# First pass over the tokens with two weight slices instead of three, weight conversions moved behind the masks of the attention pairs, q of units 1 and 3 decayed on GpSimd

## Chip, core and metric

The kernel runs on one core of one Trainium2 chip. The metric is device time in microseconds, the median of several executions. A profiled execution gives a trace of every instruction of the engines: TensorE (PE, its weight loads as PEld), VectorE (DVE), ScalarE (ACT), GpSimd (POOL) and SyncE (SP), which issues the DMAs.

## What is computed

Three layers, one behind the other, in float32:

```python
# q, k, v: (4, 8, 576, 64); x: (2304, 512) after the first layer
scores = q @ k.transpose(0, 1, 3, 2) / sqrt(64)
ret = scores * gamma[head] ** (i - j)        # for i >= j, else 0; no softmax
x = (ret @ v)                                # heads side by side: (2304, 512)
h = x @ w_in                                 # (2304, 2048)
x = (h * sigmoid(1.702 * h)) @ w_out         # (2304, 512)
h = x @ w2_in                                # (2304, 1024)
s = h * softmax(h)
out = ((s - mean(s)) / sqrt(var(s) + 1e-6) * g_ln) @ w2_out
```

## The kernel before

Every matmul of the two feed-forward layers is made of three: each operand is split into a high part (rounded to fp32r, by ScalarE) and a remainder (operand minus high part, by GpSimd or VectorE), and high x high, low x high and high x low are summed in PSUM. The weights come as 64 bit floats; VectorE turns them into 32 bit floats with three bit instructions per half slice (`convert`, lines 236, 239, 242: a shift, and two combinations), ScalarE rounds (L279 for a half, L259 for a whole slice), GpSimd subtracts (L283, L264).

**Attention.** 16 units (a batch and two heads each) run as 8 pairs `k`; at the end of pair `k` the raw weight halves and the x splits for the first block are issued. Of a pair: `scores` (L399 on PE, then the masks on VectorE, L404), `states` (L363) and `scan` (L372), `across` (L429 to L441: earlier chunks through the scanned states), `within` (L414), and `take`, which brings the result into `xb`. q has to be multiplied by powers of gamma: for units from `PLAIN` = 4 on GpSimd does it ahead (`decay_q`, L333, L338) and `take` is a ScalarE copy (L452); for units 0 to 3 `take` multiplies on VectorE instead (L457, L459), with `qdec` for even and `odec` for odd units.

**First feed-forward layer.** The 2304 tokens are five blocks `j` of 384, 512, 512, 512 and 384 columns, the hidden size is 16 slices `f` of 128. `GENS` cuts the slices into passes: in pass `g` all five blocks run through the slices of that pass, and the outputs of the passes are added up in `y`. A step (g, j, f) is an h group (`emit_h`: 12 matmuls, L496, then sigmoid on ScalarE L501, product L504, rounding L508 or L506, remainder L509) and a y group (`emit_y`: 12 matmuls, L529). PE's order is h of the next step, then y of the step before. h0_2 below is the h group of block 0 and slice 2. x of the next block is split in the last two steps of a block (`split_x`, L476 on ScalarE, L477 on GpSimd): of four parts two in the last step but one, two in the last.

**The order of background work** is written out by hand: `self.bg` is a list of pieces (conversions count 1, the roundings and remainders behind them 0); `background(n)` takes n conversions and what follows them off the list and puts them into the engines' queues at that place. In the pairs the table `(0, 0, 0, 0, 0, 1, 2, 3)[k]` and one further call say how many; in the steps `bg` and `free`. Each engine runs its queue in order, so a piece stands still when one ahead of it waits. `load_w` issues the next raw half slice on SP; `halves` is the order of the first six (slices 0, 1 and 2).

**Later.** While the first layer runs, the slices 8 to 15 and the second layer's weights are loaded, converted and split in the same way; the second layer follows.

Of the kernel before, what the change touches and what calls it, by code (L numbers as in the profile page):

```python
# [17 lines left out]
B, H, S, D = 4, 8, 576, 64  # L18
NP = H // 2
# [13 lines left out]
FH = NF // 2  # L33
GENS = ((0, 3), (3, 8), (8, 16))
STEPS = [(g, j, f) for g, lo_hi in enumerate(GENS) for j in range(NB) for f in range(*lo_hi)]
# [14 lines left out]
for _name, _w in (  # L50
    ("half", 1), ("g_ln", FB), ("vdec", NP * 3), ("step", NP), ("istep", H), ("tri2", LAST), ("tri", CH),
    ("qdec", NP * CH), ("odec", NP // 2 * CH),
):
    _CC[_name] = (_n, _n + _w)
    _n += _w
# [4 lines left out]
def constants():  # L60

    gamma = (1.0 - 2.0 ** (-5.0 - np.arange(H))).astype(np.float64)
    c = np.zeros((P, _n_consts), np.float64)

    def put(name, a):
        lo, hi = _CC[name]
        c[:, lo:hi] = a.reshape(P, hi - lo)

    qdec = np.zeros((P, NP, CH))
    odec = np.zeros((P, NP // 2, CH))  # L70
    step = np.zeros((P, NP))
    vdec = np.zeros((P, NP, 3))
    j = np.arange(P)
    for p in range(NP):

        g = gamma[2 * p + (j // D ^ p % 2)]
        qdec[:, p] = g[:, None] ** j[None, :]
        step[:, p] = g ** CH
        for a in range(2):
            vdec[:, p, a] = gamma[2 * p + a] ** (CH - j)  # L80
        vdec[:, p, 2] = g ** -(j % D)
        if p % 2:
            odec[:, p // 2] = gamma[2 * p + j // D][:, None] ** j[None, :]
    put("qdec", qdec)
    put("odec", odec)
    put("step", step)
    put("istep", np.broadcast_to(gamma ** -CH, (P, H)))

    put("vdec", vdec / math.sqrt(D))
    put("tri", (j[:, None] <= np.arange(CH)[None, :]).astype(np.float64))  # L90
    put("tri2", (j[:, None] % D <= np.arange(LAST)[None, :]).astype(np.float64))
    put("half", np.full((P, 1), -0.5))
    return c.astype(np.float32)
# [25 lines left out]
NU = 6  # L119
PLAIN = 4  # L120
EARLY = 3
# [35 lines left out]
class Build:  # L157
# [38 lines left out]
    def load_decays(self, p, n):  # L196

        lo = _CC["qdec"][0] + p * CH
        hi = lo + n * CH if p + n < NP else CCONST
        self.load(_M["c"] + lo, self.const_in[:, lo:hi])  # L200

# [124 lines left out]

    def decay_q(self, k):

        n = NCH * CH
        for u in (2 * k, 2 * k + 1):  # L330
            q = self.un(u)[0][:, CQ:CK]
            d = self.const("qdec")[:, u % NP * CH:(u % NP + 1) * CH]
            self.nc.gpsimd.tensor_tensor(q[:, n:], q[:, n:], d[:, 0:LAST], ALU.mult)  # L333
        for u in (2 * k, 2 * k + 1):
            q = self.un(u)[0][:, CQ:CK]
# [110 lines left out]
    def take(self, u, o, part):  # L446
# [3 lines left out]
        x = self.x(u)[:, n:S] if part else self.x(u)[:, 0:n]  # L450
        if u >= PLAIN:
            nc.scalar.copy(x, o[:, 0:LAST] if part else o)  # L452
            return
        p = u % NP
        d = self.const("odec")[:, p // 2 * CH:] if p % 2 else self.const("qdec")[:, p * CH:]
        if part:
# [246 lines left out]
    def run(self):  # L703
# [15 lines left out]
        for f in range(FH):  # L719
            self.wraw[f] = self.wp.tile([P, 2 * SLICE], U32, tag="w", name=f"wraw{f}", bufs=FH)  # L720
        halves = [(0, 0), (1, 0), (0, 1), (2, 0), (1, 1), (2, 1)]
        raws = halves + [(f, h) for f in range(3, FH) for h in range(2)]

# [7 lines left out]
        self.load_unit(0, 1)  # L731
        self.load_decays(0, 1)
        self.fill_scan()
        for u in range(1, NU):
            for part in range(2):
                self.load_unit(u, part)
            if u == 2:
                self.load_decays(1, NP - 1)

        for f, h in halves:  # L740
# [3 lines left out]
            self.bg += [(0, p, "split") for p in self.split_half(f, t, h)]  # L744
        for f in range(3, FH):
            t = T_START[f % 2]
# [7 lines left out]
        self.scale_v(0)  # L754
        self.scale_v(1)
        for k in range(NPAIR):
            u = 2 * k
            nxt = k + 1 < NPAIR
            early = k < EARLY
            if k + 2 < NPAIR:  # L760
                self.decay_q(k + 2)
            if nxt and not early:
# [66 lines left out]
        for g, j, f in STEPS:  # L829
# [222 lines left out]
```

## Time and profile before

| | us |
|---|---|
| median of 3 runs | 688.37 (688.34 to 688.55) |
| profiled execution | 687.97 |
| its span, first to last instruction | 686.2 |
| PE busy in the span | 666.3 (97%) |
| DVE busy | 487.6 (71%) |
| POOL busy | 250.5 (37%) |
| ACT busy | 231.8 (34%) |

The profiled execution took 687.97 us, 0.4 less than the median; 1.8 us of it lie around the span. Sums below are made against the profiled execution. A share of busy time is a mean over stages with different limits: attention takes about the first 67 us, the first feed-forward layer runs until about 480, the second until the end. Matmuls are pipelined, so a busy PE need not be at full rate: PEclk says what clock it was granted.

### The profile page before, as it was taken

Reading aid. Unit: us, or ns where it says so; the run is one execution under the profiler, and the core shown is the slowest. Engines: PE = TensorE matmul, PEld = TensorE weight load, DVE = VectorE, ACT = ScalarE, POOL = GpSimd, SP = SyncE. Lnnn points to the kernel's source line nnn. Section 1 sums busy time; section 2 is a strip of 40 time slices with the busy share of each in tenths; the row PEclk is TensorE's granted clock in tenths of the full one; section 3 lists DMA queues with packets and bytes.
Section 4 is the critical chain, followed back from the end, with each engine's and each line's share of the span. In section 5 each row is a group of like instructions: output and inputs, shape, how many; then the busy total and the mean of one; then the engine's idle time right before and its main releaser. Section 6 shows DMA issues by size and latency. Waiting matters only on the chain.

```text
span 686.2 us, 10467 instructions
## 1 busy us (share of the span) xinstructions
PE 666.3 (97%) x4086; PEld 577.0 (84%) x4086; DVE 487.6 (71%) x773; ACT 231.8 (34%) x494; POOL 250.5 (37%) x264
## 2 busy tenths in 40 slices
PE   9999779999999999999999999999999999999998
PEld 8898658899788889898888888899888888888887
DVE  3768546777978869768677676458789887877780
ACT  2554324443121114311121211155754434452331
POOL 1444624643442217912040220259943224331300
PEclk9999889999999999999999999999999999999999
DMA  8996330000212222013211110000000000000001
GB/s 334 416 399 265 124 123 1 0 2 1 90 64 93 92 93 62 0 32 96 90 62 62 62 32 0 1 1 4 1 16 1 32 32 31 32 16 16 32 31 47
DMA packets 14881, 49.48 MB, mean 72 GB/s; under 512 B 1648, under 2 KB 2288, under 8 KB 14832
## 3 DMA queue, kind: packets, MB, share of 16 engines
q1 hardware_dynamic: 14832, 48.82, 19.8%
q8 instruction: 32, 0.52, 0.3%
q14 instruction: 17, 0.14, 0.1%
HBM read 44.09 MB, written 4.72 MB: 71 GB/s over the span
## 4 chain that ended last, share of the span: by engine, by line
PE 80%; DVE 7%; issue 6%; POOL 5%; ACT 1%; POOLq 0%; DVEq 0%; ACTq 0%
PE yp L529 24%; PE h L496 24%; PE o L694 14%; PE h L603 10%; POOL xs L477 3%; POOL w L264 2%; PE zT L667 2%; PE s L399 2%; PE o L429 1%; PE o L414 1%; PE warm L714 1%; PE T L363 1%; DVE mem L404 1%; DVE mem L609 1%; DVE mem L504 1%
## 5 line engine op out<-in xcount | busy, mean ns | idle before, releaser
L529 PE MATMUL yp<-gs,w 128*128 128x512 f32 (+1 forms) x960 | 215.7, 373 | 10.3 <-ACT w L279 7.3
L496 PE MATMUL h<-xs,w 128*128 128x512 f32 (+1 forms) x960 | 214.0, 370 | 2.2 <-POOL xs L477 2.0
L529 PEld LDWEIGHTS yp<-gs,w 128*128 128x128 f32 x960 | 177.9, 191 | 35.6 <-ACT w L279 8.1
L496 PEld LDWEIGHTS h<-xs,w 128*128 128x128 f32 x960 | 176.3, 189 | 28.5 <-POOL xs L477 5.2
L477 POOL TENSOR_TENSOR xs<-xb,xs 128x384 fp32r<-128x384 f32 (+3 forms) x96 | 94.2, 1009 | 203.1 <-ACT xs L476 203.1
L501 ACT ACTIVATE mem<-h 128x512 f32<-128x512 f32 (+1 forms) x80 | 44.5, 556 | 269.9 <-PE h L496 265.4
L504 DVE TENSOR_TENSOR mem<-h,mem 128x512 f32<-128x512 f32 (+1 forms) x80 | 50.9, 636 | 101.9 <-ACT mem L501 101.8
L694 PE MATMUL o<-w,zs 128*128 128x512 f32 (+1 forms) x456 | 102.9, 382 | 0.0
L694 PEld LDWEIGHTS o<-w,zs 128*128 128x128 f32 x456 | 81.3, 188 | 15.2
L509 DVE TENSOR_TENSOR gs<-mem,gs 128x512 fp32r<-128x512 f32 (+1 forms) x80 | 68.4, 855 | 13.9 <-ACT gs L506 6.9
L264 POOL TENSOR_TENSOR w<-mem,w 128x512 fp32r<-128x512 f32 x34 | 46.0, 1381 | 36.3 <-ACT w L259 36.3
L565 POOL TENSOR_TENSOR ys_s<-mem,ys_s 128x256 fp32r<-128x256 f32 x36 | 35.1, 986 | 51.9 <-ACT ys_s L564 41.8
L508 DVE CAST gs<-mem 128x512 fp32r<-128x512 f32 (+1 forms) x69 | 38.9, 563 | 6.9 <-PE yp L529 0.5
L603 PE MATMUL h<-wt,ys_s 128*128 128x512 f32 x162 | 41.3, 390 | 0.0
L609 DVE TENSOR_TENSOR mem<-h,mem 128x512 f32<-128x512 f32 x36 | 24.6, 687 | 21.1 <-PE h L603 12.5
L603 PEld LDWEIGHTS h<-wt,ys_s 128*128 128x128 f32 x162 | 30.3, 188 | 6.2
L476 ACT CAST xs<-xb 128x384 fp32r<-128x384 f32 (+3 forms) x96 | 35.0, 433 | 0.0
L654 POOL TENSOR_TENSOR mem<-mem 128x1 f32<-128x1 f32 x18 | 10.3, 574 | 64.7 <-DVE mem L653 64.7
L404 DVE SCALAR_TENSOR_TENSOR mem<-s,mem 128x512 f32<-128x512 f32 x32 | 21.8, 739 | 9.8 <-PE s L399 9.8
L677 DVE TENSOR_TENSOR zs<-zT,zs 128x512 fp32r<-128x512 f32 x36 | 23.1, 684 | 7.7 <-ACT zs L676 7.7
L603 PE MATMUL h<-wb,ys_a 128*128 128x512 f32 x108 | 27.5, 390 | 0.3 <-ACT mem L612 0.3
L646 DVE TENSOR_TENSOR mem<-mem 128x1024 f32<-128x1024 f32 x18 | 24.8, 1375 | 3.7 <-ACT mem L644 3.7
(82 smaller groups left out, 726.0 us busy)
## 6 DMA issues: line engine op xcount, KB each, us to landing
mem<-in_att SPq DMA_DIRECT2D x16, 576.0 KB, 8.2
mem<-in_att SPq DMA_DIRECT2D x16, 544.0 KB, 9.0
wraw<-in_w SPq DMA_DIRECT2D x16, 512.0 KB, 10.0
mem<-in_w SPq DMA_DIRECT2D x16, 512.0 KB, 3.7
out<-mem SPq DMA_DIRECT2D x17, 256.0 KB, 2.0
mem<-in_w2in SPq DMA_DIRECT2D x8, 512.0 KB, 3.7
mem<-in_w2out SPq DMA_DIRECT2D x8, 512.0 KB, 3.6
mem<-in_consts SPq DMA_DIRECT2D x1, 320.0 KB, 8.9
```

The costliest lines, as they stand in the source:

```text
L264: nc.gpsimd.tensor_tensor(lo[:, c], w[:, c], f32(hi[:, c]), ALU.subtract)
L476: nc.scalar.copy(t[:, 0, done:done + n], x)
L477: nc.gpsimd.tensor_tensor(t[:, 1, done:done + n], x, f32(t[:, 0, done:done + n]), ALU.subtract)
L496: nc.tensor.matmul(h[:, 0:width], a[:, w], x[:, b, 0:width], start=(n == 0), stop=(n == 3 * KB - 1))
L501: nc.scalar.activation(g, h[:, 0:width], AF.Sigmoid, scale=1.702)
L504: nc.vector.tensor_tensor(g, h[:, 0:width], g, ALU.mult)
L508: nc.vector.tensor_copy(gs[:, 0], g)
L509: lo_engine.tensor_tensor(gs[:, 1], g, f32(gs[:, 0]), ALU.subtract)
L529: nc.tensor.matmul(o, a[:, w], gs[:, b], start=(first and i == 0), stop=(last and i == 2))
L565: nc.gpsimd.tensor_tensor(ys[:, 1], src, f32(ys[:, 0]), ALU.subtract)
L603: nc.tensor.matmul(o, a[:, l, k], m[:, w], start=(start and i == 0), stop=(stop and i == 5), skip_group_check=True,)
L694: nc.tensor.matmul(o[:, 0:n], z[:, a, k], b[:, c:c + n], start=(k == 0 and i == 0), stop=(k == FB - 1 and i == 2),)
```

## The change

The first pass takes slices 0 and 1, the second slices 2 to 7, the third 8 to 15 as before. Only the four halves of slices 0 and 1 are converted one by one, three conversions in each of the pairs 4 to 7, behind that pair's masks. In the first pass two conversions follow each h group and one each y group; the last two x parts are queued directly behind the last h group. Of units 0 to 3 only 0 and 2 are still multiplied in `take`; q of units 1 and 3 is decayed on GpSimd ahead of the pairs. `odec` goes, the decays of odd unit 1 are loaded ahead of those of unit 0. Raw slices are loaded in another rhythm (one half in pairs 2 to 5, three in pairs 6 and 7).

```diff
-GENS = ((0, 3), (3, 8), (8, 16))
+GENS = ((0, 2), (2, 8), (8, 16))
...
-PLAIN = 4
+PLAIN = (0, 2)
...
-    def decay_q(self, k):
+    def decay_q(self, *units):
...
-        if u >= PLAIN:
+        if u not in PLAIN:
             nc.scalar.copy(x, o[:, 0:LAST] if part else o)
             return
-        p = u % NP
-        d = self.const("odec")[:, p // 2 * CH:] if p % 2 else self.const("qdec")[:, p * CH:]
+        d = self.const("qdec")[:, u % NP * CH:]
...
-        halves = [(0, 0), (1, 0), (0, 1), (2, 0), (1, 1), (2, 1)]
-        raws = halves + [(f, h) for f in range(3, FH) for h in range(2)]
+        halves = [(0, 0), (1, 0), (0, 1), (1, 1)]
+        raws = halves + [(f, h) for f in range(2, FH) for h in range(2)]
...
-        self.load_decays(0, 1)
+        self.load_decays(1, 1)
         self.fill_scan()
         for u in range(1, NU):
             for part in range(2):
                 self.load_unit(u, part)
+            if u == 1:
+                self.load_decays(0, 1)
             if u == 2:
-                self.load_decays(1, NP - 1)
+                self.load_decays(2, NP - 2)
...
+        self.decay_q(1)
+        self.decay_q(3)
         for k in range(NPAIR):
...
             if k + 2 < NPAIR:
-                self.decay_q(k + 2)
+                self.decay_q(u + 4, u + 5)
...
-            self.background((0, 0, 0, 0, 0, 1, 2, 3)[k])
+            self.background((0, 0, 0, 0, 2, 2, 2, 3)[k])
...
-                self.background(k > 4)
+                self.background(k > 3)
                 self.scan(k + 1, pt)
...
-            for _ in range((0, 0, 1, 1, 2, 2, 1, 1)[k]):
+            for _ in range((0, 0, 1, 1, 1, 1, 3, 3)[k]):
                 load_w()
...
-                for _ in range(2):
+                for _ in range(3):
                     load_w()
...
-            if fl:
+            if g == 0:
+                while ahead and not start:
+                    ahead.pop(0)()
+                self.background(2)
+            elif fl:
                 self.background(bg, free)
...
-            self.background(1 if fl else 1 + bg, free and not fl)
+            if g:
+                self.background(1 if fl else 1 + bg, free and not fl)
+            else:
+                self.background(1)
```

What this does to the queues stands in the order of the built programs. In their rows `wraw1` is a raw slice, `w1` a split one, `mem` holds the converted half in between, `h0_1` is an h group's bank, `gs` its split result, `xs0_1_2` part 2 of block 1's x in pass 0.

VectorE from the end of attention on, before, from h0_0's product to h0_2's:

```order
L504 TENSOR_TENSOR mem_60<-h0_0_972,mem_60 128x384
L509 TENSOR_TENSOR gs_71<-mem_60,gs_71 128x384
L242 SCALAR_TENSOR_TENSOR mem_60<-wraw0_95 128x512
L236 TENSOR_SCALAR mem_60<-wraw2_97 128x512
L239 SCALAR_TENSOR_TENSOR wraw2_97<-wraw2_97,mem_60 128x512
L242 SCALAR_TENSOR_TENSOR mem_60<-wraw2_97 128x512
L504 TENSOR_TENSOR mem_60<-h0_1_1033,mem_60 128x384
L509 TENSOR_TENSOR gs_71<-mem_60,gs_71 128x384
L236 TENSOR_SCALAR mem_60<-wraw1_96 128x512
L239 SCALAR_TENSOR_TENSOR wraw1_96<-wraw1_96,mem_60 128x512
L242 SCALAR_TENSOR_TENSOR mem_60<-wraw1_96 128x512
L504 TENSOR_TENSOR mem_60<-h0_2_1073,mem_60 128x384
```

and with the change, from the last pair's conversions to h0_1's remainder:

```order
L231 TENSOR_SCALAR mem_60<-wraw1_96 128x512
L234 SCALAR_TENSOR_TENSOR wraw1_96<-wraw1_96,mem_60 128x512
L237 SCALAR_TENSOR_TENSOR mem_60<-wraw1_96 128x512
L498 TENSOR_TENSOR mem_60<-h0_0_985,mem_60 128x384
L503 TENSOR_TENSOR gs_71<-mem_60,gs_71 128x384
L231 TENSOR_SCALAR mem_60<-wraw2_97 128x512
L234 SCALAR_TENSOR_TENSOR wraw2_97<-wraw2_97,mem_60 128x512
L237 SCALAR_TENSOR_TENSOR mem_60<-wraw2_97 128x512
L231 TENSOR_SCALAR mem_60<-wraw2_97 128x512
L234 SCALAR_TENSOR_TENSOR wraw2_97<-wraw2_97,mem_60 128x512
L498 TENSOR_TENSOR mem_60<-h0_1_1046,mem_60 128x384
L503 TENSOR_TENSOR gs_71<-mem_60,gs_71 128x384
```

Before, the last conversion of slice 0 and all of the second halves of slices 1 and 2 stood behind the products of h0_0, h0_1 and h0_2. Now slice 1's last half stands ahead of h0_0's product, and what follows it is slice 2, which the first pass does not use.

GpSimd in the same place, before:

```order
L283 TENSOR_TENSOR w1_946<-mem_60,w1_946 128x512
L283 TENSOR_TENSOR w0_844<-mem_60,w0_844 128x512
L283 TENSOR_TENSOR w2_1018<-mem_60,w2_1018 128x512
L477 TENSOR_TENSOR xs0_1_0_1023<-xb_78,xs0_1_0_1023 128x192
L477 TENSOR_TENSOR xs0_1_0_1023<-xb_78,xs0_1_0_1023 128x320
L477 TENSOR_TENSOR xs0_1_1_1028<-xb_78,xs0_1_1_1028 128x192
L477 TENSOR_TENSOR xs0_1_1_1028<-xb_78,xs0_1_1_1028 128x320
L283 TENSOR_TENSOR w1_946<-mem_60,w1_946 128x512
L477 TENSOR_TENSOR xs0_1_2_1087<-xb_78,xs0_1_2_1087 128x192
L477 TENSOR_TENSOR xs0_1_2_1087<-xb_78,xs0_1_2_1087 128x320
L477 TENSOR_TENSOR xs0_1_3_1092<-xb_78,xs0_1_3_1092 128x192
L477 TENSOR_TENSOR xs0_1_3_1092<-xb_78,xs0_1_3_1092 128x320
```

and with the change:

```order
L278 TENSOR_TENSOR w0_697<-mem_60,w0_697 128x512
L471 TENSOR_TENSOR xs0_0_3_929<-xb_78,xs0_0_3_929 128x384
L278 TENSOR_TENSOR w1_813<-mem_60,w1_813 128x512
L471 TENSOR_TENSOR xs0_1_0_1029<-xb_78,xs0_1_0_1029 128x192
L471 TENSOR_TENSOR xs0_1_0_1029<-xb_78,xs0_1_0_1029 128x320
L471 TENSOR_TENSOR xs0_1_1_1034<-xb_78,xs0_1_1_1034 128x192
L471 TENSOR_TENSOR xs0_1_1_1034<-xb_78,xs0_1_1_1034 128x320
L471 TENSOR_TENSOR xs0_1_2_1060<-xb_78,xs0_1_2_1060 128x192
L471 TENSOR_TENSOR xs0_1_2_1060<-xb_78,xs0_1_2_1060 128x320
L471 TENSOR_TENSOR xs0_1_3_1065<-xb_78,xs0_1_3_1065 128x192
L471 TENSOR_TENSOR xs0_1_3_1065<-xb_78,xs0_1_3_1065 128x320
L259 TENSOR_TENSOR w2_1074<-mem_60,w2_1074 128x512 x2
```

The remainders of slices 0 and 1 now stand ahead of block 1's x; its eight subtractions follow each other, and slice 2's remainder comes behind them.

TensorE behind y0_0, before:

```order
L529 MATMUL yp0_0_3_1054<-gs_71,w0_844 128x384
L496 MATMUL h0_2_1073<-xs0_0_0_587,w2_1018 128x384 x3
L496 MATMUL h0_2_1073<-xs0_0_1_698,w2_1018 128x384 x3
L496 MATMUL h0_2_1073<-xs0_0_2_807,w2_1018 128x384 x3
L496 MATMUL h0_2_1073<-xs0_0_3_915,w2_1018 128x384 x3
```

and with the change:

```order
L523 MATMUL yp0_0_3_1082<-gs_71,w0_697 128x384
L490 MATMUL h1_0_1108<-xs0_1_0_1029,w0_697 128x512 x3
L490 MATMUL h1_0_1108<-xs0_1_1_1034,w0_697 128x512 x3
L490 MATMUL h1_0_1108<-xs0_1_2_1060,w0_697 128x512 x3
L490 MATMUL h1_0_1108<-xs0_1_3_1065,w0_697 128x512 x3
```

h1_0, which needs block 1's x, takes the place of h0_2.

## Rows read from the trace of the kernel before

**Rows 1.** Page, the span in 40 slices: PE's busy tenths.
```profile
PE   9999779999999999999999999999999999999998
```

**Rows 2.** Windows of 10 us: length, PE, PEld, DVE, ACT, POOL busy, clock, DMA, GB/s.
```profile
60.00:70.00 10.00, 9.27 (x114) 8.24 (x113) 8.02 (x14) 3.45 (x8) 2.52 (x3) 1.00 0.30 113
70.00:80.00 10.00, 5.25 (x24) 4.21 (x24) 5.57 (x7) 4.75 (x13) 6.25 (x8) 0.89 0.36 122
80.00:90.00 10.00, 6.97 (x23) 6.04 (x23) 5.15 (x7) 1.23 (x3) 3.23 (x4) 0.77 0.23 82
90.00:100.00 10.00, 7.86 (x25) 6.89 (x26) 3.01 (x4) 3.56 (x9) 4.03 (x5) 0.66 0.62 211
```

**Rows 3.** Waits of PE: total us, times, longest.
```profile
PE yp L529 <- ACT w L279: 7.3, 2, 4.0
PE yp L529 <- POOL w L283: 2.5, 3, 1.1
PE h L496 <- POOL xs L477: 2.0, 3, 1.3
```

**Rows 4.** Timeline, 56 to 104 us: start, length, engine, line, operation [idle before].
```profile
67.30 1.09 ACT L452 COPY xb<-o 128x512 f32<-128x512 f32 x2
...
67.34 2.37 PE L496 MATMUL h<-xs,w 128*128 128x384 f32 x12
...
75.43 1.08 DVE L236 TENSOR_SCALAR mem<-wraw 128x512 uint32<-128x512 uint32 x1
...
78.67 0.69 PE L529 MATMUL yp<-gs,w 128*128 128x384 f32 x1 [3.29 <-ACT w L279]
...
91.04 0.44 PE L529 MATMUL yp<-gs,w 128*128 128x384 f32 x1 [4.05 <-ACT w L279]
...
99.92 2.88 PE L529 MATMUL yp<-gs,w 128*128 128x512 f32 x12
```

**Rows 5.** Windows of 2 us in block 0.
```profile
74.00:76.00 2.00, 1.38 (x8) 1.06 (x7) 1.44 (x2) 0.52 (x1) 2.00 (x3) 1.00 0.00 0
...
82.00:84.00 2.00, 2.00 (x7) 2.00 (x7) 1.74 (x2) 0.00 (x0) 1.23 (x2) 0.50 0.22 88
```

**Rows 6.** Groups of 12 matmuls back to back: 512 columns (chain), 384 columns (timeline).
```profile
105.52 2.72 PE yp L529 x12
...
164.48 2.24 PE L529 MATMUL yp<-gs,w 128*128 128x384 f32 x12
...
168.64 2.24 PE L529 MATMUL yp<-gs,w 128*128 128x384 f32 x12
```

**Rows 7.** Timeline of POOL and DVE, 80 to 136 us: apart, and beside each other.
```profile
97.43 2.82 POOL L477 TENSOR_TENSOR xs<-xb,xs 128x256 fp32r<-128x256 f32 x4 [4.90 <-ACT xs L476]
...
118.14 4.16 POOL L477 TENSOR_TENSOR xs<-xb,xs 128x320 fp32r<-128x320 f32 x4
122.95 3.90 POOL L477 TENSOR_TENSOR xs<-xb,xs 128x320 fp32r<-128x320 f32 x4 [0.65 <-ACT xs L476]
132.06 2.55 POOL L264 TENSOR_TENSOR w<-mem,w 128x512 fp32r<-128x512 f32 x2 [5.22 <-ACT w L259]
...
112.45 0.43 DVE L508 CAST gs<-mem 128x512 fp32r<-128x512 f32 x1
...
113.59 0.42 DVE L236 TENSOR_SCALAR mem<-wraw 128x512 uint32<-128x512 uint32 x1
114.05 0.69 DVE L239 SCALAR_TENSOR_TENSOR wraw<-wraw,mem 128x512 uint32<-128x512 uint32 x1
...
118.64 1.17 DVE L509 TENSOR_TENSOR gs<-mem,gs 128x512 fp32r<-128x512 f32 x1
119.74 0.82 DVE L236 TENSOR_SCALAR mem<-wraw 128x512 uint32<-128x512 uint32 x1
...
125.04 1.35 DVE L242 SCALAR_TENSOR_TENSOR mem<-wraw 128x512 uint32<-128x512 uint32 x1
```

**Rows 8.** Timeline, DVE at the end of pair 0.
```profile
16.48 1.28 DVE L459 TENSOR_TENSOR xb<-o,mem 128x512 f32<-128x512 f32 x2
```

More of the change, by code (lines that the diff above doesn't have):

```diff
@@ L51 @@
     ("half", 1), ("g_ln", FB), ("vdec", NP * 3), ("step", NP), ("istep", H), ("tri2", LAST), ("tri", CH),
-    ("qdec", NP * CH), ("odec", NP // 2 * CH),
+    ("qdec", NP * CH),
 ):
@@ L69, in constants @@
     qdec = np.zeros((P, NP, CH))
-    odec = np.zeros((P, NP // 2, CH))
     step = np.zeros((P, NP))
@@ L81, in constants @@
         vdec[:, p, 2] = g ** -(j % D)
-        if p % 2:
-            odec[:, p // 2] = gamma[2 * p + j // D][:, None] ** j[None, :]
     put("qdec", qdec)
-    put("odec", odec)
     put("step", step)
@@ L198, in load_decays @@
         lo = _CC["qdec"][0] + p * CH
-        hi = lo + n * CH if p + n < NP else CCONST
-        self.load(_M["c"] + lo, self.const_in[:, lo:hi])
+        self.load(_M["c"] + lo, self.const_in[:, lo:lo + n * CH])
     def fill_scan(self):
@@ L325, in q @@
         return t[rows, CQ + c * CH:min(CQ + (c + 1) * CH, CK)]
-    def decay_q(self, k):
+    def decay_q(self, *units):
         n = NCH * CH
-        for u in (2 * k, 2 * k + 1):
+        for u in units:
             q = self.un(u)[0][:, CQ:CK]
@@ L333, in decay_q @@
             self.nc.gpsimd.tensor_tensor(q[:, n:], q[:, n:], d[:, 0:LAST], ALU.mult)
-        for u in (2 * k, 2 * k + 1):
+        for u in units:
             q = self.un(u)[0][:, CQ:CK]
@@ L744, in run @@
             self.bg += [(0, p, "split") for p in self.split_half(f, t, h)]
-        for f in range(3, FH):
+        for f in range(2, FH):
             t = T_START[f % 2]
```

## The prediction, made before the result was known

> **What bounds the kernel now.** I read the slices first: TensorE is busy nine tenths or more of nearly every slice, so little can be won except in the fifth and sixth, where it is at 7 [rows 1]. The windows put numbers on that: from 60 to 100 us TensorE is busy 9.27, 5.25, 6.97 and 7.86 us of each 10, and from 70 us on at granted clocks of 0.89, 0.77 and 0.66 [rows 2]. This is block 0 of the first pass. The list of TensorE's waits says for whom: 7.3 us for ScalarE's rounding of w (L279), 2.5 us for GpSimd's remainder of w (L283), 2.0 us for GpSimd's remainder of x [rows 3]. The timeline shows why. At 78.67 the y group of slice 1 starts after a wait of 3.29 us: the VectorE conversion of that slice's second half began only at 75.43, because in its queue it stands behind the multiplications of h0_1. At 91.04 the y group of slice 2 has waited 4.05 us, since its last conversion stands behind the multiplications of h1_0, a group that comes after it [rows 4]. After such a wait TensorE runs at 0.50 of its clock, that is at 1.2 GHz: from 82 to 84 us it is busy all the time and ends only 7 matmuls [rows 5]. So the first pass starts without its weights, and pays twice.
>
> **The size of the hole.** At 2.4 GHz a group of 12 matmuls takes 2.72 us at 512 columns, and two groups of 384 columns take 168.64 - 164.48 = 4.16 us, 2.08 each [rows 6]. Between h0_1's start at 67.34 and the end of y1_0 at 99.92 + 2.88 = 102.80 [rows 4] lie 35.46 us. In them run h0_1, y0_0, h0_2, y0_1, y0_2 (five of 2.08) and h1_0, h1_1, y1_0 (three of 2.72): 18.56 us of work. **Lost: 16.9 us.**
>
> **The change part by part.**
> 1. *Two slices in the first pass, four halves converted behind the masks of pairs 4 to 7.* All twelve conversions and the four remainders are queued ahead of h0_0's multiplications; in block 0 no y group waits for a weight any more. h0_2 and y0_2 move to the second pass, where they cost the same 4.16 us. The 16.9 us go, apart from what is late next. The conversions cost nothing on the path: pairs 4 and 5 get four more of them than before (at most 4 x 0.69 = 2.8 us, [rows 7]), in gaps where VectorE waits for the states ahead of the scan; pairs 6 and 7 have as many as before. If a gap were too short, the scan and the next pair's across would be late by at most that.
> 2. *What is late next: h1_0.* It now follows y0_0 directly and needs block 1's x, whose eight GpSimd subtractions start when ScalarE is through with the last pair: it ends its copies at 67.30 + 1.09 = 68.39 [rows 4], about 0.5 later now because w1's rounding and the sigmoid come after the conversions; plus one cast, 69.25. Four such subtractions take 2.82 us with VectorE idle and 3.90 beside its work [rows 7], so the last ends at 74.9 or 77.05, and the last matmul 0.23 later. Without waiting h1_0 would end at 67.34 + 2.08 + 2.08 + 2.72 = 74.22. New wait 0.9 to 3.1 us; I take **+3.0**, since VectorE converts slice 2 all the while.
> 3. *Blocks 1 to 4 are denser.* One whole slice is converted per block as before, but a block of 512 columns now lasts 4 x 2.72 = 10.88 us instead of 16.3. GpSimd needs 2 x 2.82 + 2.55 = 8.19 us of it alone. VectorE has five instructions a step that read or write SBUF only, 0.43 + 0.69 + 0.42 + 0.69 + 0.69 = 2.92 us alone, 5.84 a block. The two slow each other: over the two runs of four subtractions at 118.14 and 122.95 GpSimd took 8.06 us instead of 5.64, beside six such VectorE instructions (3.61 us alone), which themselves grew, 0.69 to 1.17, 0.42 to 0.82, 0.69 to 1.35 [rows 7]. So one microsecond of theirs cost GpSimd 2.42 / 3.61 = 0.67. If all of it met, a block would need 8.19 + 0.67 x 5.84 = 12.1 us, 1.2 over TensorE; block 4 (384 columns, 1.5 x 2.82 + 2.55 = 6.8, VectorE about 5.4) 10.4 against 8.32. Upper end 3 x 1.2 + 2.1 = 5.7 us, lower end 0, as the same work passed unseen in the longer blocks. I take **+3.0**, the middle: GpSimd hardly pauses, but a y group follows its h one step later, so VectorE may lag by some 3 us before TensorE sees it, and lag can be worked off in block 0 of the second pass.
> 4. *Other waits for x.* 1.3 of the 2.0 us fall at the end of the second pass's block 0, where w7's remainder stands right ahead of eight x subtractions. w7 is now ready two steps earlier. **-1.5** (0 to -2.0).
> 5. *q of units 1 and 3 on GpSimd, their takes on ScalarE.* VectorE loses two large and two small multiplications, which stand on the path between one pair's end and the next pair's masks: 1.28 us for two large ones [rows 8], so 0.6 to 0.8 per pair. ScalarE's copy now stands ahead of the v scaling, and the score matmuls of units 1 and 3 wait for GpSimd (one 512 column product, about 1.1). I take **-0.4** (-0.8 to +0.3). The 128 KB that are no longer loaded and the split load of the decays are within this.
> 6. *Raw slices.* The loads of the four halves keep their places in SP's queue or move up, and all stand behind the same x loads as before. Nothing.
>
> Sum: -16.9 + 3.0 + 3.0 - 1.5 - 0.4 = -12.8. Against the profiled execution's 687.97 that is 675.2; the median of the runs, 688.37, lies 0.4 higher: **675.6 us**. Its ends: -16.9 + 0.9 + 0 - 2.0 - 0.8 = -18.8, 669.6; -16.9 + 3.1 + 5.7 + 0 + 0.3 = -7.8, 680.6.
>
> **A rule against it.** Rows 7 show both engines slowed, each by less than the other's instruction. The Trainium skill, page "SBUF — State Buffer", section "Who interferes with whom", says that a VectorE instruction with two SBUF inputs or in a 2-port mode and a GpSimd instruction that reads SBUF exclude each other for the whole instruction. By that rule a block would take the plain sum, which is the second rival below. So far the trace agrees with the slowing and not with full exclusion (2.42 lost of 3.61).
>
> **Rivals.**
> - *The clock falls in the new wait.* For: the wait of 3.29 us before 78.67 was followed by 1.2 GHz. Against: from 74 to 76 TensorE was busy only 1.38 of 2.00 us and the clock stayed at 1.00 [rows 5], and the new wait is broken by the matmuls of each x part. Price: what the clock lost from 70 to 90 us, 10 x 0.11 + 10 x 0.23 = 3.4 us [rows 2]; once or twice, 679.0 to 682.4.
> - *GpSimd and VectorE take turns completely.* A block needs 8.19 + 5.84 = 14.0 us, 3.15 over TensorE; block 4 6.8 + 5.4 = 12.2, 3.9 over: 13.3 lost instead of 3.0, 685.9 us. For: both are to be busy without a pause. Against: the 0.67 above.
> - *Slower.* The same, but each block's wait comes in one piece and the clock falls in each of the four blocks: 685.9 + 4 x 3.4 = 699.5 us. It decides from waits of about 3 us in one piece, the size of the one at 78.67. Against: x comes in parts, so a wait of 3.15 us would be broken into three or four.
> - *The first pass still lacks weights,* a half landing after its place behind the masks; the scan behind it then waits 1 to 3 us, 677 to 679.
>
> **Chances.** Forecast 0.70, clock in the new wait 0.15, full exclusion 0.06, slower 0.04, weights late 0.03, the rest 0.02. A measurement of this kernel can tell 0.2% (1.4 us) from nothing. All but the slower case and a part of the rest lie more than that below 688.37: faster 0.95, same 0.01, slower 0.04. The range takes most of the forecast's own ends and the clock's case: 670.5 to 682.
>
> **What would show it.** Right: no wait of a y group for L279's and L283's successors in block 0; h1_0 waiting 1 to 3 us for x; clock 1.00 from 60 to 130; y1_0 ended near 84.5 us; the first pass's blocks 1 to 3 at 11 to 12 us. Wrong: GpSimd busy without a gap from 85 to 120 with TensorE below nine tenths there (step 3 too small), or a clock below 1 anywhere before 130 (the first rival), or h0_1 later than 67.4 (steps 1 and 5).

## The result, and the profile after

The changed kernel takes **677.28 us** (median of six runs, 674.60 to 679.82) against 688.46 for the one before, measured beside it: ratio of the mean times **0.9832**, 95% interval 0.9807 to 0.9856. The forecast was 675.6, its range 670.5 to 682.0. The profiled execution took 677.7 us, 10.3 less than the one before, with a span of 675.9.

The page shows the sixth slice filled and the fifth at 8 instead of 7; the third, in attention, is at 8 too. What answers to [rows 1]:

```profile
PE   9989899999999999999999999999999999999998
PEclk9999899999999999999999999999999999999999
```

The windows (columns as in [rows 2]) show what is left there: a loss from 70 to 80 with a clock below 1 up to 90, and smaller losses from 110 to 150, where before there were none.

```profile
70.00:80.00 10.00, 8.22 (x37) 6.79 (x36) 8.45 (x10) 6.14 (x17) 9.74 (x10) 0.92 0.46 158
80.00:90.00 10.00, 10.00 (x43) 8.44 (x43) 9.43 (x10) 4.27 (x10) 8.77 (x9) 0.91 0.00 0
...
110.00:120.00 10.00, 9.36 (x49) 8.28 (x48) 8.29 (x11) 5.40 (x11) 5.75 (x6) 1.00 0.00 0
120.00:130.00 10.00, 8.62 (x48) 7.92 (x47) 9.02 (x14) 3.44 (x7) 4.98 (x4) 1.00 0.00 0
```

TensorE's waits, which answer to [rows 3]: none for a weight any more, 2.1 us for x (0.73, 1.05 and 0.34, all three in the first pass), and a new kind, y groups that wait for VectorE's rounding of gs. Below them, two of its waits that no engine and no transfer is seen to end; all of these come to 3.3 us before h0_0.

```profile
PE yp L523 <- DVE gs L502: 2.6, 4, 1.0
PE h L490 <- POOL xs L471: 2.1, 3, 1.1
PE e L375 <- issue: 1.2, 1, 1.2
PE s L394 <- issue: 1.0, 1, 1.0
```

The timeline of block 0, which answers to [rows 4]: h0_1 starts at 68.77, 1.43 later than before. h1_0 (73.06) gets its last x part at 77.94. Then y0_1 runs 3.81 us for its 12 matmuls of 384 columns instead of 2.24, so mostly at 1.2 GHz. h2_0 starts at 87.41. The last row is the longest of the waits for gs, ahead of y4_0.

```profile
68.77 2.37 PE L490 MATMUL h<-xs,w 128*128 128x384 f32 x12
70.98 2.24 PE L523 MATMUL yp<-gs,w 128*128 128x384 f32 x12
73.06 2.14 PE L490 MATMUL h<-xs,w 128*128 128x512 f32 x8
75.93 0.96 PE L490 MATMUL h<-xs,w 128*128 128x512 f32 x3 [0.73 <-POOL xs L471]
77.94 0.50 PE L490 MATMUL h<-xs,w 128*128 128x512 f32 x1 [1.05 <-POOL xs L471]
78.28 3.81 PE L523 MATMUL yp<-gs,w 128*128 128x384 f32 x12
...
123.86 2.36 PE L523 MATMUL yp<-gs,w 128*128 128x384 f32 x12 [1.04 <-DVE gs L502]
```

**Where the time went.** I cut the time at four starts of matmul groups and subtract the work between them, at 2.72 and 2.08 us a group [rows 6]. From h0_1 to the group behind y1_0 the loss was 16.7 us (67.34 to 102.64, less 18.56 of work; the forecast's 16.9 counts to the end of y1_0's last matmul, 102.80); it is now 4.2 (68.77 to 87.41, less 14.40). From there to the first 512-column h group of the second pass it was 0.2 (102.64 to 174.88, less 72.0) and is 4.9 (87.41 to 148.03, less 55.68). From that group to the first matmul of the stage that follows (L597 here, L603 before) it was 5.63 and is 1.75 (174.88 to 482.11 less 301.60; 148.03 to 471.86 less 322.08). Attention costs 1.4 more. -12.5 + 4.7 - 3.9 + 1.4 = -10.3, the measured difference.

### The profile page after: what moved, and what is told of

It is laid out like the page before. It is cut to its first block, busy times and chain, and to the rows that moved or that the text cites. A ratio compares the mean times of both kernels' runs of the same rounds, so it can differ in the third digit from the quotient of the medians.

```text
span 675.9 us, 10468 instructions
## 1 busy us (share of the span) xinstructions
PE 662.6 (98%) x4086; PEld 574.9 (85%) x4086; DVE 488.1 (72%) x770; ACT 231.1 (34%) x496; POOL 254.8 (38%) x268
## 4 chain that ended last, share of the span: by engine, by line
PE 80%; DVE 7%; DMA 4%; issue 3%; POOL 3%; ACT 2%; SPq 0%; DVEq 0%; POOLq 0%; ACTq 0%
PE yp L523 25%; PE h L490 25%; PE o L688 14%; PE h L597 10%; DMA mem<-in_att 4%; PE zT L661 2%; POOL xs L471 2%; PE s L394 1%; PE o L409 1%; DVE mem L498 1%; DVE mem L237 1%; DVE mem L603 1%; PE T L358 1%; DVE gs L502 1%; DVE gs L503 1%
## 5 line engine op out<-in xcount | busy, mean ns | idle before, releaser
L523 PE MATMUL yp<-gs,w 128*128 128x512 f32 (+1 forms) x960 | 213.0, 371 | 2.9 <-DVE gs L502 2.6
L471 POOL TENSOR_TENSOR xs<-xb,xs 128x384 fp32r<-128x384 f32 (+3 forms) x96 | 95.8, 1026 | 193.6 <-ACT xs L470 193.5
L503 DVE TENSOR_TENSOR gs<-mem,gs 128x512 fp32r<-128x512 f32 (+1 forms) x80 | 66.4, 830 | 12.9 <-ACT gs L500 5.8
L259 POOL TENSOR_TENSOR w<-mem,w 128x512 fp32r<-128x512 f32 x36 | 48.6, 1374 | 49.0 <-ACT w L254 46.7
L597 PE MATMUL h<-wt,ys_s 128*128 128x512 f32 x162 | 41.3, 390 | 0.0
L603 DVE TENSOR_TENSOR mem<-h,mem 128x512 f32<-128x512 f32 x36 | 24.6, 687 | 21.1 <-PE h L597 12.5
L597 PEld LDWEIGHTS h<-wt,ys_s 128*128 128x128 f32 x162 | 30.3, 188 | 6.2
L648 POOL TENSOR_TENSOR mem<-mem 128x1 f32<-128x1 f32 x18 | 10.3, 572 | 64.8 <-DVE mem L647 64.8
L254 ACT CAST w<-mem 128x1024 fp32r<-128x1024 f32 x18 | 18.8, 1050 | 30.5 <-DVE mem L237 24.1
L597 PE MATMUL h<-wb,ys_a 128*128 128x512 f32 x108 | 27.6, 391 | 0.3 <-ACT mem L606 0.3
```

The lines of the kernel that those rows point to most:

```text
L259: nc.gpsimd.tensor_tensor(lo[:, c], w[:, c], f32(hi[:, c]), ALU.subtract)
L471: nc.gpsimd.tensor_tensor(t[:, 1, done:done + n], x, f32(t[:, 0, done:done + n]), ALU.subtract)
L503: lo_engine.tensor_tensor(gs[:, 1], g, f32(gs[:, 0]), ALU.subtract)
L523: nc.tensor.matmul(o, a[:, w], gs[:, b], start=(first and i == 0), stop=(last and i == 2))
L597: nc.tensor.matmul(o, a[:, l, k], m[:, w], start=(start and i == 0), stop=(stop and i == 5), skip_group_check=True,)
```

## The experiments

All of them change the changed kernel, except where it is said. "Block 0" below is the time from h0_1's start to h2_0's less 14.40 us of work; "blocks 1 to 4" the time from h2_0 to the first 512-column h group of the second pass less 55.68. Both are read from each kernel's profiled execution. The kernels were run in several sessions, each with the kernel before beside them (its medians were 688.46 to 689.21), so two rows are best compared by their ratios.

| kernel | median us | ratio of means to before, interval | h0_1 starts | lost in block 0 | lost in blocks 1 to 4 |
|---|---|---|---|---|---|
| changed | 677.28 | 0.9832 (0.9807 to 0.9856) | 68.77 | 4.2 | 4.9 |
| the same again | 676.86 | 0.9821 (0.9798 to 0.9844) | 68.34 | 2.7 | 6.3 |
| q undone | 677.46 | 0.9832 (0.9810 to 0.9855) | 68.85 | 4.2 | 4.9 |
| early conversions undone | 684.52 | 0.9934 (0.9915 to 0.9952) | 68.27 | 7.8 | 8.5 |
| no conversion in block 0 | 681.08 | 0.9885 (0.9864 to 0.9907) | 66.01 | 1.5 | 12.3 |
| remainders of w left out | 673.24 | 0.9779 (0.9763 to 0.9794) | 66.52 | 4.2 | 1.8 |
| w split later | 675.70 | 0.9807 (0.9790 to 0.9823) | 68.58 | 4.2 | 3.7 |
| w split later, x shared | 675.83 | 0.9804 (0.9780 to 0.9827) | 68.07 | 0.3 | 7.5 |
| gs rounded by ScalarE, first pass | 678.49 | 0.9847 (0.9820 to 0.9875) | 68.38 | 2.7 | 6.7 |
| gs rounded by ScalarE, from block 3 | 678.06 | 0.9850 (0.9833 to 0.9867) | 67.45 | 2.7 | 7.1 |
| the same, w split later | 678.80 | 0.9854 (0.9840 to 0.9867) | 68.79 | 2.7 | 6.9 |

### The same kernel again

Nothing is edited.

> The changed kernel once more, nothing edited. What differs between two profiles of it is chance. In the first one attention ended 1.4 us later than before (h0_1 starts at 68.77 instead of 67.34), and TensorE's waits that no engine and no transfer ends ('issue') came to 3.3 us before h0_0 instead of 1.9. Theory A (chance: these waits fall where TensorE's instructions are fetched among the saturated loads): h0_1 starts anywhere from 67.0 to 69.5, the 'issue' waits move with it, and the rest of the span, from h0_1 to the end, is the same within 0.5 us. Theory B (the change itself made attention slower): h0_1 starts at 68.8 within 0.2 again. Median between 676.5 and 678.

Theory A in part: h0_1 at 68.34 instead of 68.77, the span 675.2, so 606.9 us from h0_1 to the end instead of 607.1. What I had not expected stands in block 0 (timeline of TensorE, then the windows from 80 us):

```profile
77.49 0.50 PE L490 MATMUL h<-xs,w 128*128 128x512 f32 x1 [1.05 <-POOL xs L471]
77.83 2.25 PE L523 MATMUL yp<-gs,w 128*128 128x384 f32 x12
...
100.59 0.49 PE L490 MATMUL h<-xs,w 128*128 128x512 f32 x1 [1.01 <-POOL xs L471]
```

```profile
80.00:90.00 10.00, 9.70 (x43) 7.69 (x42) 9.54 (x11) 3.73 (x9) 8.30 (x9) 1.00 0.00 0
90.00:100.00 10.00, 9.58 (x43) 7.51 (x41) 7.86 (x9) 5.40 (x14) 9.98 (x10) 1.00 0.00 0
```

h1_0 waits as long as before, yet this time the clock stays at 1.00 and y0_1 takes 2.25 us. So block 0 loses 1.5 us less; but h2_0 and h3_0 now wait for x, h3_0 1.01 us in one piece, and blocks 1 to 4 lose 1.4 more. **Between these two profiles the clock's fall cost at most 0.2 us in the end** (9.2 us lost from h0_1 to the second pass with it, 9.0 without): what paces blocks 1 to 3 is GpSimd. The times alone can't show it that finely: of the eleven runs of this kernel the four with a mean granted clock below 1.00 took 676.86 to 679.82 (median 677.30), the seven at 1.00 674.60 to 677.68 (median 676.62). GpSimd's timeline shows how it sets the pace:

```profile
69.83 7.61 POOL L471 TENSOR_TENSOR xs<-xb,xs 128x192 fp32r<-128x192 f32 x8 [1.70 <-ACT xs L470]
77.41 2.99 POOL L259 TENSOR_TENSOR w<-mem,w 128x512 fp32r<-128x512 f32 x2
80.35 7.95 POOL L471 TENSOR_TENSOR xs<-xb,xs 128x256 fp32r<-128x256 f32 x8
90.02 2.55 POOL L259 TENSOR_TENSOR w<-mem,w 128x512 fp32r<-128x512 f32 x2 [1.72 <-PE yp L523]
92.53 8.01 POOL L471 TENSOR_TENSOR xs<-xb,xs 128x320 fp32r<-128x320 f32 x8
102.25 2.55 POOL L259 TENSOR_TENSOR w<-mem,w 128x512 fp32r<-128x512 f32 x2 [1.71 <-PE yp L523]
```

A block's round on GpSimd is 8.0 us of x, 1.7 of idleness, 2.55 of w: 12.2, where TensorE needs 10.88. The idleness carries TensorE's name, but the remainder starts when ScalarE's rounding of w has ended (88.89 + 1.05 = 89.94), which began when VectorE's last conversion of the slice had (87.64 + 1.22 = 88.86); the next block's x stands behind it.

```profile
87.64 1.22 DVE L237 SCALAR_TENSOR_TENSOR mem<-wraw 128x512 uint32<-128x512 uint32 x1
```

```profile
88.89 1.05 ACT L254 CAST w<-mem 128x1024 fp32r<-128x1024 f32 x1 [4.14 <-DVE mem L237]
```

From block 4 on the picture is another: between h4_0's start (109.13 here, 109.74 in the first profile) and the end of the stretch 4.3 and 4.4 us are lost, so most of what the table gives for blocks 1 to 4. There the y groups wait 2.5 and 2.6 us for VectorE, whose instructions were stretched from 106 to 110 us in the repeat (1.23 to 1.50 each for L237, L231 and L234), and GpSimd stands idle 4.2 us ahead of w's remainder. The two engines are late in turn.

### q of units 1 and 3 undone, and q alone

```diff
-PLAIN = (0, 2)
+PLAIN = 4
...
-        self.decay_q(1)
-        self.decay_q(3)
```

(and the table odec with its load back, as before the change).

> The changed kernel with q of units 1 and 3 as before (VectorE applies the decay when it takes the outputs; the 128 KB table is loaded again). The prediction gave this part -0.4 us. Theory A (attention is paced by the x loads and by TensorE's 'issue' waits, so the two takes are off the path): no change beyond chance, 676.5 to 678.0. Theory B (GpSimd's q ahead of the score matmuls, or the other order of the loads, cost the 1.4 us): h0_1 back at 67.3 and 675.9. The prediction's own: 677.7.

677.46 us and h0_1 at 68.85: nothing is seen of q, theory A. The other way round, the kernel before with the q part alone:

> The kernel before with nothing but the q part of the change: q of units 1 and 3 decayed by GpSimd, their outputs copied by ScalarE, the 128 KB table not loaded. The prediction's term: -0.4, so a ratio of 0.9994 to before. Theory now (attention is paced by loads and by TensorE's 'issue' waits; it ended anywhere from 61.2 to 64.7 in nine profiles with the same attention): no difference that the runs can show, ratio within 0.998 to 1.002. Rival (the q part makes attention 1 to 1.4 us longer, as the first profile of the change suggested): ratio 1.002 or more.

687.74 us beside 689.00, ratio 0.9986 (0.9973 to 0.9998): -1.0 us, between -0.1 and -1.9. The rival, that q cost attention its 1.4 us, is out; the term of -0.4 lies in the interval. What moves attention's end lies elsewhere. In ten profiles whose pairs are the changed kernel's (one has the old q, the nine others the same loop over the pairs) h0_0 started between 61.20 and 64.66; with the old conversions at 63.16 (before) and 63.72 (q alone). The earliest, at 61.20, is that of the kernel without conversions in block 0, whose attention is instruction for instruction that of the changed kernel; it had 0.3 us of waits by "issue" where the first profile had 3.3. Before had 1.9:

```profile
PE s L399 <- issue: 1.0, 1, 1.0
PE e L380 <- issue: 0.9, 1, 0.9
```

So 1.3 of the 1.4 us of the first comparison are these waits, and come and go. They are not all of the scatter: the kernel with the remainders of w left out had 2.5 us of them and started h0_0 at 62.34.

### The early conversions undone

```diff
-            self.background((0, 0, 0, 0, 2, 2, 2, 3)[k])
+            self.background((0, 0, 0, 0, 0, 1, 2, 3)[k])
...
-                self.background(k > 3)
+                self.background(k > 4)
```

> The two-slice first pass stays; the conversions behind the masks go back to the places they had before (pair 5: one, pair 6: two and one, pair 7: three and one), so slice 1 is not ready with the pairs. Theory (the early conversions cost attention nothing and are what lets block 0 begin with its weights): h0_0 starts where it did with them, 61 to 65 as in the other runs; h0_1 and y0_0 wait again for w, 2 to 5 us more in block 0, of which part comes back since GpSimd is the late one afterwards: 678 to 681. Rival (with two slices the weights are in time anyway, and the conversions in pairs 4 and 5 only delay the scans): 675.5 to 677.

684.52 us, 7.2 to 7.7 more than the two medians of the change: the theory's direction, and about twice its size. h0_0 started at 64.08, where the ten others lie, so the conversions did cost attention nothing that can be seen. The waits of TensorE behind h0_0:

```profile
PE yp L523 <- ACT mem L529: 4.4, 3, 2.7
PE h L490 <- POOL xs L471: 3.5, 2, 2.9
PE yp L523 <- POOL w L278: 0.7, 1, 0.7
```

Only 0.7 us are waits for a weight. The late conversions push block 1's x (2.9 us in one piece) and ScalarE's copies of y (L529), which stand behind roundings of w; the clock was at 0.92, 0.73 and 0.83 in the windows 70 to 80, 80 to 90 and 120 to 130, so up to 5.2 us are lost by it, where the changed kernel loses up to 1.7. The two-slice pass without the early conversions keeps only 4.5 of the 11 us.

### No conversion in block 0

```diff
                 while (f, 0) not in self.split:
                     self.background(1)
-                self.background(1)
...
-                self.background(2)
+                self.background((0, 3, 3, 2, 2)[j])
...
-                self.background(1)
+                self.background(j > 0)
```

> No conversion of slice 2 while block 1's x is subtracted (none in block 0's two steps; four instead of three per step in blocks 1 and 2; the rest later). Theory (VectorE's conversions slow GpSimd): the eight subtractions take 0.70 us each instead of 0.95, the last ends near 75.9, h1_0 waits 0.4 us instead of 2.5, TensorE's clock stays at 1.00 from 70 to 90 and y0_1 takes 2.1 us instead of 3.7: 3.7 us less, of which up to 1.5 come back as VectorE's lag in blocks 1 to 4, so 674 to 675. Rival (GpSimd is that slow by itself, or has the wait from ScalarE's casts): the wait stays at 2 to 2.5 us and the clock falls again: 677 to 678. Third (the wait goes, the clock falls all the same): 675.5.

681.08 us: the theory held in block 0, in its direction, and its sum failed behind it. GpSimd's groups, 67 to 75 us in this kernel and 69 to 78 in the repeat of the changed one (mean ns of one behind the busy time):

```profile
L471 POOL TENSOR_TENSOR xs<-xb,xs 128x320 fp32r<-128x320 f32 x4 | 3.8, 953 | 0.0
L471 POOL TENSOR_TENSOR xs<-xb,xs 128x192 fp32r<-128x192 f32 x4 | 2.4, 602 | 1.7 <-ACT xs L470 1.7
```

```profile
L471 POOL TENSOR_TENSOR xs<-xb,xs 128x320 fp32r<-128x320 f32 x4 | 4.9, 1216 | 0.0
L471 POOL TENSOR_TENSOR xs<-xb,xs 128x192 fp32r<-128x192 f32 x4 | 3.0, 757 | 1.7 <-ACT xs L470 1.7
```

Without VectorE's conversions beside them the eight subtractions take 6.2 us instead of 7.9 by these rows, h1_0 loses 1.3 us (70.30 to 74.33) instead of 2.5, and the clock stays at 1.00. But the conversions put off to blocks 1 and 2, four a step, lose 12.3 us there, where three a step lost 4.9 and 6.3. h3_0 shows it, and ScalarE beside it:

```profile
96.15 0.73 PE L490 MATMUL h<-xs,w 128*128 128x512 f32 x2 [1.77 <-ACT xs L470]
99.63 1.65 PE L490 MATMUL h<-xs,w 128*128 128x512 f32 x3 [2.75 <-POOL xs L471]
```

```profile
93.96 1.05 ACT L254 CAST w<-mem 128x1024 fp32r<-128x1024 f32 x1 [4.39 <-DVE mem L237]
94.91 0.59 ACT L495 ACTIVATE mem<-h 128x512 f32<-128x512 f32 x1
95.40 2.14 ACT L470 CAST xs<-xb 128x320 fp32r<-128x320 f32 x6
```

ScalarE stood idle for 4.39 us ahead of w's rounding, with the x that h3_0 needed queued behind it. The clock fell behind these waits (the windows from 90, 100 and 120 us):

```profile
90.00:100.00 10.00, 5.48 (x23) 3.96 (x22) 8.08 (x10) 3.58 (x8) 7.56 (x8) 0.88 0.00 0
100.00:110.00 10.00, 9.64 (x34) 7.26 (x34) 6.62 (x9) 4.01 (x8) 6.42 (x6) 0.78 0.01 2
...
120.00:130.00 10.00, 8.99 (x42) 8.81 (x43) 6.45 (x10) 5.83 (x13) 4.60 (x4) 0.83 0.00 0
```

Up to 1.2 + 2.2 + 1.7 = 5.1 of the 12.3 us are the clock's, so what the denser conversions cost by themselves is not shown.

### The remainders of w left out

GpSimd's subtraction is replaced for slices 2 to 7 by a copy of w on ScalarE, so the low parts of these weights are not computed.

```diff
-            nc.gpsimd.tensor_tensor(lo[:, c], w[:, c], f32(hi[:, c]), ALU.subtract)
+            if key in range(2, FH):
+                nc.scalar.copy(lo[:, c], w[:, c])
+            else:
+                nc.gpsimd.tensor_tensor(lo[:, c], w[:, c], f32(hi[:, c]), ALU.subtract)
```

> The remainders of slices 2 to 7 are left out: ScalarE copies w in their place, twelve copies of 128x512 in all, so GpSimd has 12 x 1.37 = 16 us less to do in the first pass and at its end. Theory (GpSimd and VectorE together are overfull in blocks 1 to 4 of the first pass): VectorE's instructions there go back toward 0.69 and 0.42 us, y groups no longer wait for VectorE nor h groups of blocks 2 to 4 for x; 3 to 4.5 us less, 672.5 to 674. Rival (not the work but the order: x's roundings on ScalarE still stand behind w's rounding, which waits for VectorE): at most 1.5 us less. h1_0's wait of 2.5 us stays in both.

673.24 us, 3.6 to 4.0 less than the two medians of the change (2.9 to 3.7 by the ratios), and blocks 1 to 4 lose 1.8 instead of 4.9: the theory. VectorE's conversions from 85 to 125 us, in the repeat and then here:

```profile
L237 DVE SCALAR_TENSOR_TENSOR mem<-wraw 128x512 uint32<-128x512 uint32 x7 | 7.7, 1106 | 0.0
L234 DVE SCALAR_TENSOR_TENSOR wraw<-wraw,mem 128x512 uint32<-128x512 uint32 x7 | 6.5, 932 | 0.2
...
L231 DVE TENSOR_SCALAR mem<-wraw 128x512 uint32<-128x512 uint32 x7 | 5.2, 747 | 0.0
```

```profile
L237 DVE SCALAR_TENSOR_TENSOR mem<-wraw 128x512 uint32<-128x512 uint32 x8 | 6.7, 835 | 0.0
L234 DVE SCALAR_TENSOR_TENSOR wraw<-wraw,mem 128x512 uint32<-128x512 uint32 x8 | 6.2, 781 | 0.3
...
L231 DVE TENSOR_SCALAR mem<-wraw 128x512 uint32<-128x512 uint32 x8 | 4.3, 537 | 0.0
```

With GpSimd lighter, VectorE's own instructions get 0.15 to 0.27 us shorter each. Alone they take 0.69, 0.69 and 0.42 [rows 7].

### w split later

Each slice's rounding and remainder are queued behind the next three conversions, so behind two parts of the next x; the order of GpSimd's queue is then four x subtractions, w, four x subtractions.

```diff
-            self.bg += [(1, p) for p in pieces]
-            self.bg += [(0, p, "split") for p in self.split_weight(f, t)]
+            self.bg += [(1, p) for p in pieces[:3]]
+            self.bg += held_split
+            self.bg += [(1, p) for p in pieces[3:]]
+            held_split = [(0, p, "split") for p in self.split_weight(f, t)]
```

> Each slice's rounding (ScalarE) and remainder (GpSimd) are queued three conversions later, that is behind the next block's first two x parts, so that neither waits for VectorE's last conversion with x standing behind it. Nothing is left out. In the repeat of the changed kernel GpSimd waits 1.7 us ahead of two such remainders between 77 and 105 us and works without a pause else; h groups wait 1.65 us for x in blocks 2 to 4 of the first pass, and 2.5 in block 1. Theory (GpSimd sets the pace of blocks 1 to 3 and loses 1.7 us per block in its own queue): both waits and the later waits for x go, 1.5 to 2.5 us less, 674.5 to 675.5. Rival (the sum of GpSimd's work with VectorE's collisions sets the pace: what it does not wait it works longer): no change within 0.7 us of 677.

675.70 us, 1.2 to 1.6 under the two medians of the change, though the intervals overlap; in the profile blocks 1 to 4 lose 3.7 instead of 4.9, with the clock's fall in block 0 as there. No h group of blocks 2 to 4 waits for x any more. So the order in the queues is worth about 1 us of the loss. Leaving the remainders out was worth about 3, but it takes their wait in GpSimd's queue away too, so the two don't simply add.

### x shared between GpSimd and VectorE

On top of the last edit VectorE subtracts two of the four parts of block 1's x, and two conversions of block 0 are left for later.

```diff
-            nc.gpsimd.tensor_tensor(
+            engine = nc.vector if (gen, j) == (0, 1) and k > 1 else nc.gpsimd
+            engine.tensor_tensor(
...
-                self.background(2)
+                self.background(0 if start and not fl else 2)
```

> w's rounding and remainder three conversions later, as in the run that was 1 us faster between h0_1 and the second pass; besides VectorE subtracts parts 2 and 3 of block 1's x (four subtractions, GpSimd does four instead of eight), and two conversions of block 0 are left for later. Theory (in the first pass GpSimd is the fuller engine, so what is taken from it at the start counts): h1_0 waits 0 to 0.8 us instead of 2.5, no fall of the clock, and 1.5 to 3 us less up to the second pass than with eight: 672.5 to 674.5. Rival (GpSimd and VectorE are one budget, four subtractions on VectorE cost as much lag there): the wait goes, but y groups of blocks 2 to 4 wait longer for VectorE: 675 to 676.5.

675.83 us: the rival. h1_0 does not wait at all, and the clock stays at 1.00:

```profile
72.35 2.92 PE L491 MATMUL h<-xs,w 128*128 128x512 f32 x12
75.11 2.27 PE L524 MATMUL yp<-gs,w 128*128 128x384 f32 x12
...
86.67 0.50 PE L491 MATMUL h<-xs,w 128*128 128x512 f32 x1 [0.86 <-POOL xs L472]
```

Block 0 loses 0.3 us instead of 4.2, and blocks 1 to 4 lose 7.5 instead of 3.7: all but 0.2 of it comes back, as waits for x from h2_0 on.

### gs rounded by ScalarE

```diff
-                    g, j, f, nc.vector, start or (last_block and not have_next), ahead if start else ()
+                    g, j, f, nc.vector, g == 0 or (last_block and not have_next), ahead if start else ()
```

> In the first pass ScalarE rounds gs in every block, not in block 0 alone, so VectorE has 0.56 us (512 columns) or 0.42 (384) less in each of eight steps. Theory (VectorE is the late one in the first pass's last blocks: y groups wait 2.6 us for its rounding, and h groups are held up by its products): these waits go, 2 to 3 us less, 674.5 to 675.5. Rival (the lag is set by GpSimd and VectorE slowing each other, so VectorE works faster only as far as GpSimd gets slower, and x comes later): the y groups' waits turn into waits of h groups for x, 676.5 to 678.

678.49 us. The y groups' waits for VectorE are gone, and as the rival said the h groups wait instead, 5.9 us in all where it was 2.1 and, in the repeat, 3.4:

```profile
PE h L490 <- POOL xs L471: 5.9, 8, 1.1
```

```profile
98.53 4.05 POOL L471 TENSOR_TENSOR xs<-xb,xs 128x320 fp32r<-128x320 f32 x4 [2.25 <-ACT xs L470]
```

But not as I had put it: GpSimd is not slower, it is idle 2.25 us ahead of x. ScalarE's rounding of gs waits for VectorE's product, and the roundings of x stand behind it. The same edit from block 3 of the first pass to block 0 of the second only, and that with w split later:

```diff
-                    g, j, f, nc.vector, start or (last_block and not have_next), ahead if start else ()
+                    g, j, f, nc.vector, start or (g == 0 and j > 2) or (g == 1 and j == 0) or (last_block and not have_next), ahead if start else ()
```

> ScalarE rounds gs in blocks 3 and 4 of the first pass and block 0 of the second alone, where y groups wait 2.5 us for VectorE, and not in blocks 1 and 2, where x was late when all blocks had it. Theory (these waits are VectorE's lag): they go, x is as before there, 2 to 2.5 us less, 674.5 to 675.3. Rival (ScalarE's rounding waits for VectorE's product, and x's roundings stand behind it): the waits turn into waits for x as in the run with all blocks, no gain, 676.5 to 678.

> Both edits: w's rounding and remainder three conversions later, and gs rounded by ScalarE from block 3 of the first pass to block 0 of the second. If the two lose in different places (x in blocks 1 to 3, VectorE's lag from block 4 on) their gains add: 3.5 to 4.5 us less than the changed kernel, 672.8 to 673.8. If one of them only moves the wait, the sum is that of the other alone.

678.06 us is the rival again: the y groups' waits go and x is late. In that profile the clock was at 0.83 from 110 to 120, which is up to 1.7 of its 7.1 us. 678.80 us is neither of the two cases expected: it is not the later split alone, 675.70, but 3.1 above it (the intervals of the ratios lie apart). The two edits do not add; where ScalarE has to wait for VectorE, x is late, in both also once behind the stretches of the table, 0.86 us in the second pass.

## Why the prediction was right, and where its sizes were not

The direction, the place and the main term were right, and the time is 1.7 us above the forecast.

**Step 1** (-16.9, no y group waits for a weight in block 0): so it was; the list of waits names none. The run with the early conversions undone shows that they carry about 7 us of the gain, and that pairs 4 and 5 hide them, as far as the scatter of attention's end lets one see.

**Step 2** (+3.0, h1_0 waits for block 1's x, 0.9 to 3.1): 2.5 us were lost in it (73.06 to 78.28, less 2.72). The contention that I put into it is real: 6.2 us without conversions, 7.6 to 7.9 beside them. But the last subtraction ended at 77.89 instead of 77.05, mostly since h0_1 and all before it were later. **The first rival** came with it in one profile and not in the other: the clock fell to 1.2 GHz behind h1_0's wait, for 1.6 us in y0_1 instead of the 3.4 priced, and was then worth 0.2 at most in these two profiles, since the repeat without it lost nearly as much behind.

**Step 3** (+3.0, blocks 1 to 4 too dense for GpSimd and VectorE) is the term that was mis-sized: 4.7 more than before, and 6.1 in the repeat, where the bound was 5.7. The mechanism was the one named: with some 16 us less for GpSimd (12 remainders of 1.37, an estimate from the page's mean) the loss falls to 1.8, and VectorE's lag came to be seen by TensorE, in the 2.5 to 2.6 us of waits for gs. I took the middle since VectorE could lag unseen and GpSimd "hardly pauses". It does pause: 1.7 us a round, ahead of w's remainder, which waits for VectorE through ScalarE with x behind it. That wait was not in the sum (a queue's order, not its work), and the later split puts it at about 1 us in all.

**Step 4** (-1.5, other waits for x): all such waits from the second pass on are gone, and the stretch up to the next stage loses 3.9 us less. Too small by 2.4, in the change's favour.

**Step 5** (-0.4, q): -1.0 by itself (-0.1 to -1.9), so not refuted. The profile showed +1.4 for all of attention, and that is chance, since the same attention ended up to 3.4 us apart. A term of 0.4 cannot be read from one profile here, nor 1.4 us from a few runs, as the forecast assumed: the six runs of the changed kernel lie 5.2 us apart. **Step 6** (nothing) was not tried by itself.

By size: steps 1 and 2 missed by +1.4 (the clock's 1.6, the 0.2 by which the hole was smaller, and 0.1 in h0_1, less the 0.5 by which h1_0's wait was smaller), step 3 by +1.7, step 4 by -2.4, step 5 by +1.8. Together +2.5, from -12.8 to -10.3. That the time came so near owes something to their cancelling. Two of the forecast's own signs of being wrong were there: a clock below 1 before 130 us, and h0_1 later than 67.4. And y1_0 made way for h2_0 at 87.4 instead of ending near 84.5.

**The rival of full exclusion** (685.9 us) did not come. In the repeat, from h2_0's start to h4_0's (85.40 to 109.13, blocks 2 and 3), GpSimd did 16.6 us of work at the lengths its instructions have with no such work of VectorE beside them (1.27 for a remainder of w; 1.00, 0.87, 0.73 and 0.60 for an x subtraction of 384, 320, 256 and 192 columns), and VectorE 11.0 us of conversions, roundings and remainders with operands in SBUF alone, at theirs (0.69, 0.69 and 0.42 for the three of a conversion, 0.43 for a rounding, 0.69 for a remainder). Instructions at the edges count by their share. That is 27.6 us of work in 23.7; 1.35 of it is only that neighbouring records of one engine lap over each other. By the rule of the Trainium skill (page "SBUF — State Buffer", section "Who interferes with whom") the two would have shut each other out for whole instructions and not fitted; this trace shows both slowed, and at least 2.5 us of overlap. The same section says that a cast or an operation with a scalar can contend too, with its one input, where it runs in a 2-port mode; there the trace agrees (L231, 0.42 alone, 0.75 beside GpSimd's work and 0.54 with less of it). **The slower case** did not come either: no wait behind h1_0 is longer than 1.04 us, and the clock stayed at 1.00 from 90 on. It took waits of about 3 us in one piece as its condition, but the clock fell behind h1_0's 0.73 and 1.05 us as well.

## What to carry to other kernels

When one engine's stall is taken out of a stage, look up at once which helper engine's round per block is nearest to the time that is left, and sum its queue with the waits in it, not its work alone: here 8.0 + 1.7 + 2.55 us against 10.88. From then on a gain anywhere else in the stage, be it 1.6 us of clock or 2.5 us of a wait, may come back in the next blocks, as it nearly did here. Look at both helpers: GpSimd was the late one up to block 3, VectorE behind it. And a helper that waits for a late one delays everything that is queued behind it, so work with a far due time belongs behind work with a near one (worth about 1 us here, not clear of the runs' noise).

## What the chip showed besides

The same wait (0.73 and 1.05 us before the last two parts of h1_0) was followed by 1.2 GHz in four of the eight profiles that have it, and by the full clock in the other four, the changed kernel being among both. What decides it stays open.

Attention's end scatters by 3.4 us with the same instructions. TensorE's waits by "issue" are a large part of that (0.3 us in the earliest profile, 3.4 in the latest), and fall while the loads keep the DMA engines full (share 1.0 from 10 to 60 us). In the thirteen profiles there are 43 of them ahead of h0_0, and every one ended 2.2 to 2.5 us after a transfer of 16 KB on the instruction queue had begun: the longest at 40.64 to 42.88 and 59.77 to 62.05 in the changed kernel, 39.60 to 42.00 and 58.34 to 60.62 before. That they wait for TensorE's own instructions among the loads is likely, but no run here was made to show it.
